# State-space convolution and gated MLP in one kernel: the opening stage in a new order, with the modulation vectors made by other matrix products

## The chip, the cores and the metric

The kernel runs on one core of one Trainium2 chip. The metric is the device time of one execution in microseconds, as the median of the runs. A core has a matrix engine (TensorE, PE in the profile, with its weight loads shown apart as PEld), a vector engine (VectorE, DVE), an activation engine (ScalarE, ACT), GpSimd (POOL) and SyncE (SP), whose queue issues most of the transfers here. Each engine runs its own instructions in order. Results of TensorE go to PSUM, from where VectorE or ScalarE takes them to SBUF.

## The reference

One sequence of L = 2048 positions and D = 640 channels goes through a block of two branches.

```python
mod = (silu(c) @ w_mod).reshape(6, 640)          # c is 1 x 640, w_mod 640 x 3840
sa, ca, ga, sb, cb, gb = mod
h = layernorm(x) * (1 + ca) + sa
P = exp(dt * A * l);  K = real(sum_n C * P * dB)  # 640 channels, 128 states, 2048 positions
x = x + ga * (causal_convolution(h, K) + h * Dskip)
h = layernorm(x) * (1 + cb) + sb
x = x + gb * ((silu(h @ w1) * (h @ w3)) @ w2)     # w1, w3: 640 x 1728
```

All of it is float32.

## The kernel before, in words

The program has three stages. In the **front** (0 to about 138 us of the span) everything is made that the convolution starts from. In the **rounds** (to about 380 us) the convolution's kernel for 16 channels at a time (a "step", 40 of them) is generated beside the Fourier transforms of u. Then follows the gated MLP, which is almost pure TensorE work. The change touches the front, and one addition in the first ten steps.

**What the front makes.** Eight blocks of the matrix `w_mod` (256 columns each, the last 128) give the vectors sa, ca and ga. A word `wl+i` of the list below loads block i, `ms+i` multiplies it with silu(c), and `mc+i` puts the result as columns (one channel per partition) into `cols`. In before, `ms` has silu(c) as the stationary operand and lets the 256 columns of the block stream past, in four column groups of TensorE at once. The result is a row, which VectorE copies to SBUF (`uk<-pm`), and `mc` turns it into columns by a product with a stationary piece of that row (`pm<-one`), which VectorE copies again (`cols<-pm`). From the columns `SA`, `SB`, `SC` and `SD` make the constant that the layer norm's shift adds to u (`rrow`, `shift`), and `MG`, `MH` make the gate.

The 16 tiles of x (`xl+j` loads one) get their layer norm (`LS`, statistics of two tiles on VectorE and four tiny operations on GpSimd; `LN`, the scaling, on ScalarE), and the first Fourier step (`U+j`, products of x with a constant matrix into two PSUM tiles `pu`). `V0+j` and `V1+j` take the two halves out, add the shift, and `V1+j` stores the tile's u to DRAM (`us<-u`). In before, for even j, TensorE adds the shift itself in the first half (products with `rrow`) and ScalarE copies that half; VectorE adds the shift in all others. The PSUM tile of the first half has one buffer, named Z.

For each step s: `PA`, `PQ` (products `pa<-r,lx`) make exponents, `XA`, `XQ` their exponential on ScalarE, `PH` phases on GpSimd (two steps at a time), `AB`, `CO`, `SI` their cosine and sine on ScalarE, `E1`, `E2`, `A1`, `A2` tables on VectorE, `kg` the kernel's pieces by TensorE into `pk`, `K` their way out on VectorE with Dskip added in one small operation (`pk<-pk,dz`) and the gate multiplied in, `pt` and `uk` its first Fourier step. `R1` to `R8` turn the parameters of channels 128 to 639 into logarithms and phases, with wide operations on VectorE and ScalarE; `dp` loads these parameters.

**The end of the front.** When all of u is in DRAM, eight transfers (`ul+0` to `ul+3`, `uk<-us`) bring the first 128 channels back with position and frequency exchanged, `st+10` multiplies them (`p<-uk,s`), ScalarE copies a part (`kc`), and VectorE's product `T` begins the rounds. `CL` closes the front's pools and loads the first constants of the rounds.

**What sets the order.** In the front each engine and SP's queue keep the order in which the list `FRONT` names the words, 264 of them; the list is written out by hand. The rounds follow a second list that stays as it is. A pool with one buffer adds waits: `pm` uses the PSUM banks pb and pk in turn, so a block's products wait until the copy of an earlier block has read its bank.

Of the kernel before, what the change touches and what calls it, by code (L numbers as in the profile page):

```python
# [17 lines left out]
P = 128  # L18
# [7 lines left out]
SPC = DC // SD  # L26
NS = D // SD
# [86 lines left out]
def tile_kernel(ctx: ExitStack, tc: tile.TileContext, a):  # L114
# [54 lines left out]
    V.memset(dz, 0.0)  # L169
    sc = kp.tile([P, KD], F32, name="sc")  # L170
# [17 lines left out]
    rrow = pm_.tile([P, D], F32, name="rrow")  # L188
# [168 lines left out]
    def mod_first(i):  # L357

        w = wm.pop(i)
        n = w.shape[2]  # L360
        pm = psS.tile([P, 512], F32, name="pm", tag=("pb", "pk", "pb", "pk", "pb", "pb", "pk", "pb")[i], bufs=1)
        mod_sums(w, pm)
        part = flat[2 * (i % 2)][:, 6 * D:]
        V.tensor_copy(part[:, :n], pm[:, :n])
        pms[i] = pm, part, n

    def mod_cols(i):

        pm, part, n = pms.pop(i)
# [6 lines left out]
    def shift_a():  # L376
# [114 lines left out]
    def u_products(j):  # L491
# [3 lines left out]
        for h in range(2):  # L495
            one = j % 2 == 0 and h == 0
            for q in range(2 if one else 0):
                for hh in range(2):
                    PE.matmul(pus[h][hh * 64:hh * 64 + 64, q, :320], c1[q * NA:q * NA + 1],
                              rrow[q * NA:q * NA + 1, hh * 320:hh * 320 + 320],  # L500
                              start=True, stop=False, tile_position=(q * NA, hh * 64))
            for q in range(2):
                r0 = (2 * h + q) * NA
                r = slice(r0, r0 + NA)
                for hh in range(2):
                    PE.matmul(pus[h][hh * 64:hh * 64 + 64, q, :320], s1r[r], x[r, hh * 320:hh * 320 + 320],
                              start=not one, stop=True, tile_position=(r0, hh * 64))

    def u_out(j, h):
# [108 lines left out]
    def kgen(s):  # L618
        E, A = EC.pop(s), AA.pop(s)
        pk = psS.tile([P, SD // 4, NB], F32, name="pk", tag="pk", bufs=1)  # L620
        for g in range(SD // 4):
            for st, x in enumerate((E, A)):
                for dq in range(4):
                    keep(PE.matmul(pk[dq * 32:dq * 32 + 32, g, :], x[:, g * 4 + dq, 1, :], x[:, g * 4 + dq, 0:3:2, :],
                                   start=(st == 0), stop=(st == 1), tile_position=(0, dq * 32)))
# [26 lines left out]
    def u_load(ch, i):  # L652

        fs = slice(i * 8, i * 8 + 8)
        for h in range(2):
            lo, hi = max(ch * DC, h * 320), min(ch * DC + DC, h * 320 + 320)
            if lo < hi:
                for c in range(2):
                    nc.sync.dma_start(uk[c * 64:c * 64 + 64, 0, fs, lo - ch * DC:hi - ch * DC],
                                      usr[h, c, :, fs, lo - h * 320:hi - h * 320])  # L660
# [200 lines left out]
    def small_loads():  # L861

        Q.dma_start(s1, a["s1"])
        Q.dma_start(i2, a["i2"])
        Q.dma_start(dz[NA - 8:P:NA], a["D"].rearrange("o (g q) -> (o q) g", q=4))

# [4 lines left out]
              "V1": lambda k: u_out(k, 1), "SA": once_only(shift_a), "SB": once_only(shift_b), "SC": once_only(shift_c),  # L871
# [6 lines left out]
              "ul": lambda k: u_load(0, k)}  # L878
    FRONT = (
# [695 lines left out]
```

## Time and profile before

| | us |
|---|---|
| runs | 950.4, 954.11, 955.71 |
| median | 954.11 |
| profiled execution | 954.98 |
| its span, first to last instruction | 952.8 |
| mean granted TensorE clock over the span | 0.955 |

All times below are those of the profiled execution, counted from the start of its span. Its own time is 2.2 us longer than the span, and 0.9 us above the median.

A row of the stretch view gives, for each engine, how long it was busy in that stretch and with how many instructions, then the clock granted to TensorE (1.00 is full speed), the share of the DMA engines and their rate. Timeline rows give start, duration, engine, operation, what is written from what, and in brackets how long the engine stood idle before it and who released it. One float32 matmul of the program stands in the trace as two records, so 15 products show as 30. The trace has no clock record before 28 us; the column shows 1.00 there for lack of one.

### The profile page before, as it was taken

The page shows a single profiled execution, that of the slowest core. Times are in us where ns is not written, and L with a number is a line of the kernel's source. Part 1 is how long each engine was busy: PE and PEld are TensorE (multiplying, and loading weights), DVE is VectorE, ACT ScalarE, POOL GpSimd, SP SyncE. Part 2 cuts the span into 40 slices and gives each one's busy share as a digit, 9 for nine tenths or more (in the row PEclk, how much of TensorE's full clock was granted, in tenths as well). Part 3 has the DMA queues.
Part 4 walks back from the last instruction along what each step waited for, and adds up shares of the span by engine and source line. Part 5 has one row for each costly group of instructions (what it writes and reads, how often), then busy time and mean ns, then how long its engine had stood idle before and what let it go on. Part 6 is the DMA issues. An engine that isn't in the chain of part 4 may idle for free.

```text
span 952.8 us, 20012 instructions
## 1 busy us (share of the span) xinstructions
PE 879.5 (92%) x7950; PEld 669.8 (70%) x7950; DVE 710.2 (75%) x1232; ACT 538.9 (57%) x737; POOL 269.0 (28%) x293
## 2 busy tenths in 40 slices
PE   3687979999998898999999999999999999999997
PEld 2453556666666664678888887578888888888786
DVE  5999979999999957577666665587976666664674
ACT  5877989999999632455333332466533333333332
POOL 3423345444544211133222201230242222200241
PEclk9867579999999998899999999999999999999999
DMA  8455397667675877782111116955321311123252
GB/s 267 149 170 195 153 230 208 170 180 195 195 224 153 231 219 255 203 262 83 42 56 56 56 62 191 248 199 171 126 70 55 111 56 56 56 82 98 97 189 87
DMA packets 104048, 140.68 MB, mean 148 GB/s; under 512 B 21044, under 2 KB 63156, under 8 KB 103956
## 3 DMA queue, kind: packets, MB, share of 16 engines
q1 hardware_dynamic: 93172, 113.58, 39.8%
q10 hardware_dynamic: 8480, 18.09, 5.9%
q0 software_dynamic: 2304, 7.74, 2.6%
q8 instruction: 62, 1.02, 0.4%
q14 instruction: 30, 0.25, 0.1%
HBM read 107.92 MB, written 31.46 MB: 146 GB/s over the span
## 4 chain that ended last, share of the span: by engine, by line
PE 68%; DVE 13%; ACT 7%; DMA 4%; SPq 3%; issue 3%; POOL 1%; ACTq 0%; DVEq 0%; POOLq 0%
PE ps L108 49%; PE p L108 6%; SPq L108 3%; PE pz L108 3%; PE pt L108 3%; PE pk L108 2%; PE pa L108 2%; DVE uk L108 2%; DVE u L108 2%; DVE st L108 2%; DVE E L108 1%; DVE A L108 1%; PE pu L108 1%; PE pm L108 1%; ACT A L108 1%
## 5 line engine op out<-in xcount | busy, mean ns | idle before, releaser
L108 DVE TENSOR_TENSOR s<-ps,s 128x512 f32<-128x512 f32 x138 | 94.8, 687 | 82.3 <-PE ps L108 81.6
L108 ACT CAST gh<-rw 128x640 fp32r<-128x640 f32 x87 | 63.3, 728 | 128.0 <-PE ps L108 86.4
L108 DVE TENSOR_TENSOR gl<-rw,gh 128x640 fp32r<-128x640 f32 x87 | 78.7, 904 | 69.1 <-ACT gh L108 69.1
L108 POOL TENSOR_TENSOR S<-rw 128x256 f32<-128x256 f32 x46 | 36.3, 791 | 234.3 <-DVE S0l L108 158.5
L108 PE MATMUL p<-uk,s 128*64 128x256 f32 x640 | 81.1, 397 | 16.3 <-DVE Y L108 4.0
L108 PE MATMUL ps<-xA,gh 128*128 128x512 f32 x280 | 87.6, 391 | 0.4 <-ACT xA L108 0.4
L108 PE MATMUL ps<-gh,uh 128*128 128x512 f32 x224 | 87.6, 391 | 0.0
L108 POOL TENSOR_TENSOR ph<-thi,iota 128x1376 int32<-128x1376 int32 x20 | 51.1, 2554 | 129.1 <-DVE A L108 114.0
L108 PE MATMUL ps<-gl,uh 128*128 128x512 f32 x224 | 87.3, 390 | 0.0
L108 PE MATMUL ps<-gh,ul 128*128 128x512 f32 x208 | 81.1, 390 | 0.0
L108 DVE TENSOR_TENSOR E<-A,cs 128x1024 f32<-128x1024 f32 (+1 forms) x80 | 76.5, 973 | 0.0
L108 PEld LDWEIGHTS p<-uk,s 128*64 128x64 f32 x640 | 46.6, 140 | 40.4 <-issue 7.7
L108 ACT ACTIVATE A<-pa 128x1024 f32<-128x1024 f32 (+1 forms) x80 | 64.6, 815 | 14.7 <-PE pa L108 14.6
L108 PEld LDWEIGHTS ps<-xA,gh 128*128 128x128 f32 x280 | 52.3, 188 | 12.9 <-ACT xA L108 1.0
L108 DVE TENSOR_TENSOR A<-A,ph 128x1024 f32<-128x1024 f32 x40 | 54.1, 1357 | 0.9
L108 PE MATMUL ps<-xA,gl 128*128 128x512 f32 x140 | 54.5, 390 | 0.0
L108 PE MATMUL pt<-s,K 128*64 128x128 f32 x640 | 47.4, 294 | 3.4 <-ACT uk L108 3.3
L108 PE MATMUL pz<-Y,i 64*128 64x128 f32 x640 | 47.3, 288 | 3.4 <-DVE T L108 1.8
L108 PEld LDWEIGHTS pz<-Y,i 64*128 64x128 f32 x640 | 39.6, 190 | 14.3 <-issue 8.4
L108 PE MATMUL pa<-r,lx 32*128 32x512 f32 (+1 forms) x160 | 34.5, 480 | 15.9 <-DVE u L108 9.0
L108 PEld LDWEIGHTS ps<-gl,uh 128*128 128x128 f32 x224 | 42.1, 188 | 9.0
L108 PEld LDWEIGHTS ps<-gh,uh 128*128 128x128 f32 x224 | 42.1, 188 | 8.9 <-DVE h L108 0.2
(211 smaller groups left out, 2181.1 us busy)
## 6 DMA issues: line engine op xcount, KB each, us to landing
rw<-in_w_dram ACTq DMA_DIRECT2D x44, 320.0 KB
us<-u SPq DMA_DIRECT2D x16, 640.0 KB
s<-in_s_dram SPq DMA_DIRECT2D x40, 256.0 KB
i<-in_i_dram SPq DMA_DIRECT2D x40, 256.0 KB
rw<-in_wg_dram SPq DMA_DIRECT2D x31, 320.0 KB
rw<-in_wu_dram SPq DMA_DIRECT2D x28, 320.0 KB
uk<-us SPq DMA_DIRECT2D x32, 256.0 KB
zs<-zt SPq DMA_DIRECT2D x32, 256.0 KB
```

What stands on the lines that cost most here:

```text
L108: ins = fn(*args, **kw)
```

## The change

The modulation blocks become stationary: for each 128 columns of a block and each of the five 128-row pieces of `w_mod`, one product has that 128x128 piece as its weights and one column of silu(c) as the moving operand. Ten such products per block (five for the last) leave the columns in PSUM directly; the row, its copy and the turning products go. The shift is added by VectorE alone in all 32 halves of u, and `rrow`, its copy and its products go; so does the word `SB`. In steps 0 to 9 Dskip is added by one more product into `pk` (`pk<-dz,dsel`) in place of VectorE's small addition. u is loaded in two pieces: `ul+0` to `ul+3` bring the positions of tiles 0 to 13, and a new word `ub` brings those of tiles 14 and 15, for all frequencies, in two transfers; the second set of round constants is loaded behind it. And the list is another one throughout.

```diff
-        mod_sums(w, pm)
-        part = flat[2 * (i % 2)][:, 6 * D:]
-        V.tensor_copy(part[:, :n], pm[:, :n])
-        pms[i] = pm, part, n
+        for b in range(n // P):
+            for k in range(KD):
+                PE.matmul(pm[:, b:b + 1], w[:, k, b * P:b * P + P], sc[:, k:k + 1], start=(k == 0), stop=(k == KD - 1))
+        pms[i] = pm, n
...
-        for b in range(n // P):
-            PE.matmul(pm[:, 256 + b:257 + b], part[:, b * P:(b + 1) * P], one4, start=True, stop=True)
-        V.tensor_copy(cols.rearrange("p s k -> p (s k)")[:, 2 * i:2 * i + n // P], pm[:, 256:256 + n // P])
+        V.tensor_copy(cols.rearrange("p s k -> p (s k)")[:, 2 * i:2 * i + n // P], pm[:, :n // P])
...
-        pr = sh["pr"] = psS.tile([P, 2, 512], F32, name="pr", tag="Z", bufs=1).rearrange("p a b -> p (a b)")
-        for k in range(KD):
-            PE.matmul(pr[:64, k * P:(k + 1) * P], r[:, k:k + 1].broadcast_to([P, 64]), ident, start=True, stop=True)
-
-    def shift_b():
-        V.tensor_copy(rrow[:64], sh["pr"][:64, :D])
...
-        if h == 0 and j % 2 == 0:
-            acopy(to, pu[:, :, :320])
-        else:
-            V.tensor_tensor(to, pu[:, :, :320], bc(shift, 1, 2), op=OP.add)
+        V.tensor_tensor(to, pu[:, :, :320], bc(shift, 1, 2), op=OP.add)
...
+        if s < EARLY:
+            keep(PE.matmul(pk[:, :, 0], dsel[:4], dz4[:4, s * 4:s * 4 + 4], start=False, stop=True,
+                           skip_group_check=True))
...
-        keep(V.tensor_tensor(pk[:, :, 0], pk[:, :, 0], dz[:, s * 4:s * 4 + 4], op=OP.add))
+        if s >= EARLY:
+            keep(V.tensor_tensor(pk[:, :, 0], pk[:, :, 0], dz[:, s * 4:s * 4 + 4], op=OP.add))
...
+    UB = 4 * 14
+
+    def u_last():
+
+        for c in range(2):
+            Q.dma_start(uk[c * 64 + UB:c * 64 + 64, 0], usr[0, c, UB:, :, :DC])
+        ahead[0, 1, "s2"] = stage2_load(1)
+        for i in range(2):
+            ahead[0, i, "i1"] = inverse1_load(i)
...
-              "ul": lambda k: u_load(0, k)}
+              "ul": lambda k: u_load(0, k, UB), "ub": lambda k: u_last()}
...
-        "PH+0 PA+0 xl+0 wl+0 PH+2 wl+4 ms+0 xl+7 wl+1 XA+0 ms+1 XA+1 PQ+0 xl+1 xl+6 mc+0 LS+0 XQ+0 wl+2 mc+1 "
+        "wl+3 xl+0 PA+0 PH+0 wl+2 xl+1 dp+0 wl+0 XA+0 XA+1 wl+1 wl+4 xl+5 ms+2 PQ+0 XQ+0 xl+4 mc+2 ms+3 XQ+1 "
```

How the queues move shows at three places. **TensorE, from its first instruction on** (`pT`, `pa` are exponents, `pm` the modulation blocks, `pr` and `ps` the shift). Before:

```order
L108 MATMUL pT<-ident,lt 128x128 x4
L108 MATMUL pa<-r_95,lx 128x512 x4
L108 MATMUL pm<-uk,sc 32x256 x4
L108 MATMUL pm<-uk,sc 32x128 x2
L108 MATMUL pm<-uk,sc 32x256 x4
L108 MATMUL pm<-uk,sc 32x128 x2
L108 MATMUL pa<-r_96,lx 128x256 x4
L108 MATMUL pm<-one_80,uk 128x1 x4
```

After, from the same place:

```order
L109 MATMUL pT<-ident,lt 128x128 x4
L109 MATMUL pa<-r_98,lx 128x512 x4
L109 MATMUL pm<-sc,uk 128x1 x10
L109 MATMUL pa<-r_99,lx 128x256 x4
L109 MATMUL pm<-sc,A 128x1 x10
L109 MATMUL pm<-sc,uk 128x1 x10
L109 MATMUL pa<-r_98,lx 128x512 x4
L109 MATMUL pm<-sc,A 128x1 x10
L109 MATMUL pm<-sc,uk 128x1 x10
L109 MATMUL pa<-r_99,lx 128x256 x4
L109 MATMUL pm<-sc,uk 128x1 x5
L109 MATMUL ps<-ident,u 64x128 x2
```

The blocks come in the order 2, 3, 0, 4, 1, 7 and then 6 and 5, and 55 products of one moving column now stand ahead of the shift's `ps`.

**VectorE, from the first modulation result on** (`cols<-pm` is a word `mc`, `st` and `mv` are layer norm statistics, `uk<-uk` 128x512 the `R` words, `E<-A,cs` tables). Before:

```order
L108 COPY uk<-pm 128x256 x2
L108 COPY cols<-pm 128x2
L108 BN_STATS st_218<-x 128x6 x2
L108 BN_AGGR mv_219<-st_218 128x2
L108 BN_STATS st_218<-x 128x6 x2
L108 BN_AGGR mv_219<-st_218 128x2
L108 COPY cols<-pm 128x2
L108 COPY uk<-pm 128x256
```

After:

```order
L109 COPY cols<-pm 128x2
L109 BN_STATS st_242<-x 128x6 x2
L109 BN_AGGR mv_243<-st_242 128x2
L109 BN_STATS st_242<-x 128x6 x2
L109 BN_AGGR mv_243<-st_242 128x2
L109 TENSOR_TENSOR uk<-uk 128x512 x6
L109 COPY cols<-pm 128x2 x2
L109 TENSOR_TENSOR E<-A,cs 128x16x64 x2
L109 SCALAR_TENSOR_TENSOR uk<-uk 128x512
L109 TENSOR_TENSOR uk<-uk 128x512
L109 SCALAR_TENSOR_TENSOR uk<-uk 128x512
L109 RECIPROCAL uk<-uk 128x512
```

The wide row copies are gone, `R1` to `R3` have moved up between the column copies, and each column copy still waits for its block on TensorE.

**SP's queue at the end of the front** (`us<-u` stores u, `uk<-us` loads it back, `s` and `i` are constants of the rounds). Before:

```order
L108 DMA us<-u 128x1280 x7
L667 DMA s_1253<-in_s_dram 128x512
L673 DMA i_1255<-in_i_dram 128x512
L667 DMA s_1257<-in_s_dram 128x512
L673 DMA i_1259<-in_i_dram 128x512
L659 DMA uk<-us 64x8x128 x8
```

After:

```order
L109 DMA us<-u 128x1280 x6
L657 DMA s_1264<-in_s_dram 128x512
L109 DMA uk<-us 56x8x128 x2
L109 DMA uk<-us 8x32x128 x2
L657 DMA s_1316<-in_s_dram 128x512
L663 DMA i_1318<-in_i_dram 128x512
L663 DMA i_1320<-in_i_dram 128x512
L109 DMA uk<-us 56x8x128 x6
```

One constant, the first 56 partitions of eight frequencies, and then the two transfers of the last tiles stand ahead of everything else.

More of the change, by code (lines that the diff above doesn't have):

```diff
@@ L26 @@
 SPC = DC // SD
+EARLY = SPC + 2
 NS = D // SD
@@ L169, in tile_kernel @@
     V.memset(dz, 0.0)
+    dz4 = kp.tile([P, D // 4], F32, name="dz4")
+    dsel = kp.tile([P, P], F32, name="dsel")
+    V.memset(dsel[:4], 0.0)
     sc = kp.tile([P, KD], F32, name="sc")
@@ L187, in tile_kernel @@
     pm_ = pre.enter_context(tc.tile_pool(name="pm_", bufs=1, side="right"))
-    rrow = pm_.tile([P, D], F32, name="rrow")
     shift = pm_.tile([P, D // 2], F32, name="shift")
@@ L361, in mod_first @@
         pm = psS.tile([P, 512], F32, name="pm", tag=("pb", "pk", "pb", "pk", "pb", "pb", "pk", "pb")[i], bufs=1)
[L362 to L365 removed]
+        for b in range(n // P):
+            for k in range(KD):
+                PE.matmul(pm[:, b:b + 1], w[:, k, b * P:b * P + P], sc[:, k:k + 1], start=(k == 0), stop=(k == KD - 1))
+        pms[i] = pm, n
     def mod_cols(i):
[L369 to L372 removed]
+        pm, n = pms.pop(i)
+        V.tensor_copy(cols.rearrange("p s k -> p (s k)")[:, 2 * i:2 * i + n // P], pm[:, :n // P])
     sh = {}
@@ L495, in u_products @@
         for h in range(2):
[L496 to L501, printed above, removed]
             for q in range(2):
@@ L506, in u_products @@
                     PE.matmul(pus[h][hh * 64:hh * 64 + 64, q, :320], s1r[r], x[r, hh * 320:hh * 320 + 320],
-                              start=not one, stop=True, tile_position=(r0, hh * 64))
+                              start=True, stop=True, tile_position=(r0, hh * 64))
     def u_out(j, h):
@@ L624, in kgen @@
                     keep(PE.matmul(pk[dq * 32:dq * 32 + 32, g, :], x[:, g * 4 + dq, 1, :], x[:, g * 4 + dq, 0:3:2, :],
-                                   start=(st == 0), stop=(st == 1), tile_position=(0, dq * 32)))
+                                   start=(st == 0), stop=(st == 1 and s >= EARLY), tile_position=(0, dq * 32),
+                                   skip_group_check=s < EARLY))
+        if s < EARLY:
+            keep(PE.matmul(pk[:, :, 0], dsel[:4], dz4[:4, s * 4:s * 4 + 4], start=False, stop=True,
+                           skip_group_check=True))
         PK[s] = pk
@@ L650, in tile_kernel, with u_load @@
     Pq, Yq, Zq = {}, {}, {}
-    def u_load(ch, i):
+    def u_load(ch, i, nb=NB):
         fs = slice(i * 8, i * 8 + 8)
@@ L658, in u_load @@
                 for c in range(2):
[L659 to L660 removed]
+                    Q.dma_start(uk[c * 64:c * 64 + nb, 0, fs, lo - ch * DC:hi - ch * DC],
+                                usr[h, c, :nb, fs, lo - h * 320:hi - h * 320])
     ahead = {}
@@ L911, in tile_kernel @@
     lx_out((0,))
+    V.tensor_copy(one4, one4m)
+    V.tensor_copy(dsel[:4, NA - 8:P:NA], toq[:4, NA - 8:P:NA])
     for word in FRONT:
@@ L916, in tile_kernel @@
             xw = fp.tile([P, 4 * D], F32, name="xw", bufs=1)
-            for i in range(2):
-                ahead[0, i, "s2"] = stage2_load(i)
-                ahead[0, i, "i1"] = inverse1_load(i)
+            ahead[0, 0, "s2"] = stage2_load(0)
         elif name in fronts:
```

4 lines of the change are left out of this document (2 added, 2 removed), and 26 rows, old and new, of the table FRONT.

## The prediction

> **What bounds the kernel now.** I read the page first. TensorE is the busiest engine over the whole span, but its first slices are not full, and the clock row shows it throttled there:
>
> ```profile
> PE 879.5 (92%) x7950; PEld 669.8 (70%) x7950; DVE 710.2 (75%) x1232; ACT 538.9 (57%) x737; POOL 269.0 (28%) x293
> PEclk9867579999999998899999999999999999999999
> ```
>
> The change lies in the first six slices of 23.8 us, so the table by stretch comes next (PE, PEld, DVE, ACT, POOL, then the granted clock):
>
> ```profile
> 16.39:30.00 13.61, 12.81 (x92) 7.89 (x92) 8.60 (x25) 11.89 (x11) 12.83 (x15) 1.00 0.93 296
> 16.39:121.75 105.36, 84.94 (x1088) 51.82 (x1088) 97.07 (x174) 86.73 (x87) 43.52 (x53) 0.71 0.50 174
> 121.75:138.06 16.31, 11.77 (x198) 8.83 (x198) 12.26 (x17) 13.27 (x15) 7.70 (x4) 0.69 1.09 233
> 138.06:300.00 161.94, 150.01 (x2865) 107.36 (x2862) 154.03 (x253) 152.36 (x155) 77.22 (x36) 1.00 0.68 192
> ```
>
> From the first exponent (16.39) to the last piece of u (121.75) VectorE is busy for 97.07 of 105.36 us and TensorE for 84.94: VectorE is the bound, idle for 8.3 us, of which 13.61 - 8.60 = 5.0 fall before 30 us. In the rounds behind 138.06, VectorE, ScalarE and TensorE are all over 92% busy in fixed orders, so I carry a shift of the front's end on one to one. The chain of waits shows that end:
>
> ```profile
> 120.22 1.54 DVE u L108 x2
> 121.79 3.61 DMA us<-u
> 126.17 7.25 DMA uk<-us
> 133.72 3.70 PE p L108 x16
> 138.06 0.70 DVE T L108
> ```
>
> The last store, the loads behind it and a slow `st+10` put 16.3 us between VectorE's last u and its `T`; only 12.26 of them are work for it.
>
> So the time is: VectorE's work up to the last u, plus its idle time, plus the tail. I take these in turn.
>
> **VectorE's work.** The groups of instructions up to 145 us give the prices (count, busy time, mean ns):
>
> ```profile
> L108 DVE TENSOR_TENSOR u<-pu,shift 128x640 f32<-128x640 f32 x24 | 18.7, 809 | 1.5 <-PE pu L108 1.5
> L108 DVE COPY uk<-pm 128x256 f32<-128x256 f32 x7 | 2.9, 417 | 3.9 <-PE pm L108 3.8
> L108 DVE COPY rrow<-pr 64x640 f32<-64x640 f32 x1 | 0.8, 807 | 0.0
> L108 DVE TENSOR_TENSOR pk<-pk,dz 128x4 f32<-128x4 f32 x11 | 1.8, 161 | 1.6 <-PE pk L108 1.5
> L108 DVE TENSOR_TENSOR K<-pk,gaT 128x256 f32<-128x256 f32 x11 | 4.7, 424 | 0.4
> L108 DVE BATCH_NORM_STATS2 st<-x 128x6 f32<-128x320 f32 x32 | 13.7, 469 | 0.0
> L108 DVE BATCH_NORM_AGGREGATE mv<-st 128x2 f32<-128x12 f32 x16 | 3.3, 209 | 1.0
> L108 DVE RECIPROCAL uk<-uk 128x512 f32<-128x512 f32 x1 | 3.4, 3352 | 0.0
> L108 ACT COPY u<-pu 128x640 f32<-128x640 f32 x8 | 5.5, 690 | 0.5 <-PE pu L108 0.4
> ```
>
> Gone: seven row copies and an eighth half as wide (7.5 x 0.417 = 3.1), `rrow` (0.8), and Dskip in the six steps taken out before the last u (6 x 0.16 = 1.0): 4.9 us. New: eight halves of u (8 x 0.77, half of the 1.54 of the pair above, = 6.2), and `K` of step 6, which moves ahead of the last u (0.4): 6.6. Net **+1.7**. ScalarE loses 8 x 0.69 = 5.5 us, but was idle for 18.6 of 105.36 us already; I count nothing for it. Dskip's ten products go on TensorE, which has 20 us of slack in this stretch, and cost nothing while it has; what they cost without it is in the third rival.
>
> One gain is hidden in the order. `SA` is a chain of tiny operations on five elements, and in before it falls beside GpSimd's wide `PH` of step 2:
>
> ```profile
> 28.60 3.54 POOL L108 TENSOR_TENSOR ph<-thi,iota 128x1376 int32<-128x1376 int32 x1
> 29.96 2.42 DVE L108 TENSOR_SCALAR cols<-cols 128x5 f32<-128x5 f32 x2
> 33.15 1.40 DVE L108 TENSOR_TENSOR cols<-cols 128x5 f32<-128x5 f32 x1
> 4.23 0.17 DVE L108 TENSOR_SCALAR sc<-sc 128x5 f32<-128x5 f32 x1 [3.10 <-ACT sc L108]
> ```
>
> Three operations take 3.8 us where 0.17 each would do (the 4.23 row). In the new list `PH` of step 2 stands behind `SA`. The gain lies between 0 (another chain falls beside `PH` instead) and 3.3; I take **-2.5**, nearer the row.
>
> **TensorE's first 45 us, and VectorE's idle time.** This is the term that decides. A product with a 128x128 stationary piece and one moving column is already in the trace, as `pm<-one`. In time order, TensorE's rows:
>
> ```profile
> 16.39 0.80 PE L108 MATMUL pa<-r,lx 32*128 32x512 f32 x4 [1.56 <-DVE lx L108]
> 19.82 0.58 PE L108 MATMUL pa<-r,lx 32*128 32x256 f32 x4
> 20.34 1.87 PE L108 MATMUL pm<-one,uk 128*128 128x1 f32 x8
> 20.34 1.78 PEld L108 LDWEIGHTS pm<-one,uk 128*128 128x128 f32 x8 [0.22 <-issue]
> 36.79 1.71 PE L108 MATMUL ps<-ident,u 128*64 128x128 f32 x12
> 43.16 0.61 PE L108 MATMUL pm<-one,uk 128*128 128x1 f32 x4
> 46.37 2.11 PE L108 MATMUL pu<-x,misc 32*64 32x320 f32 x16
> ```
>
> Its price is the weight load: 1.78 / 8 = 0.22 us a record at the early, slow clock, 0.61 / 4 = 0.15 at the fast one. A block is now 20 records: 4.45 us slow, 3.0 fast. Which clock holds? The table by stretches that follow the throttle's own steps of 3.41 us:
>
> ```profile
> 17.84:21.25 3.41, 3.41 (x29) 2.14 (x23) 0.85 (x2) 2.12 (x4) 3.25 (x4) 1.00 0.57 152
> 21.25:24.67 3.42, 3.42 (x23) 2.11 (x24) 3.14 (x11) 3.39 (x4) 3.26 (x3) 1.00 0.99 320
> 48.56:51.97 3.41, 3.41 (x16) 3.34 (x16) 3.38 (x3) 3.39 (x3) 0.00 (x0) 0.50 0.56 130
> 51.97:55.39 3.42, 2.41 (x32) 1.57 (x34) 3.38 (x8) 2.23 (x5) 0.00 (x0) 1.00 0.30 113
> 110.00:113.41 3.41, 3.41 (x34) 1.69 (x36) 3.41 (x5) 2.94 (x6) 1.31 (x3) 0.50 0.48 192
> ```
>
> TensorE was busy without a gap in the first two (their 1.00 is only the missing record), and the products in them still cost 0.22. It was as busy in the step from 110.00 at 0.50. The step from 48.56, all 128-column products through the whole array, was followed by 1.00. So a full busy row does not release the clock; columns that stream through the array seem to, and the new products stream one. I take the slow clock for all eight blocks.
>
> Then I walk TensorE's new order. Block 2 ends at 17.1 + 4.45 = 21.6, exponents 0.58, block 3 at 26.6, block 0 at 31.0, exponents 0.80, block 4 at 36.3, block 1 at 40.7, exponents, block 7 (half) at 43.5, the shift's `ps` at 45.5. VectorE beside it, with 0.3 us from an end on TensorE to a copy: idle from 16.6 to 21.9 (5.3). `LS+0` is 4 x 0.43 + 2 x 0.2 = 2.1 and `R1` 3.9 (six wide operations at 0.66), until 28.2; idle until block 0 at 31.3 (3.1). Two tables at 1.2 and `R2`, `R3` (0.66 x 4 + 3.35 = 6.0) last until 39.8; idle until 41.0 for block 1 (1.2). `SA`, `SC`, `LS+2`, `A1+1` and the shift's copy fill until 47.4, when the first product of u stands. The two first tiles of u hold TensorE until 50.4, block 6 until 54.9, the third tile until 57.0, block 5 until 61.4: VectorE waits 1.5 for that tile and 3.0 for block 5. That is 14.1; I add 1.4 for two small waits behind it, for the gate and the next u: 15.5 us, against 5.0 until 30 us and 0.5 from there to 60 in before. With the later 2.8 kept on both sides: **+10.0**. Bounds: +0.5 when the clock is released early (first rival), +13 when each of the three largest waits is one more us.
>
> The `dp` load, 1536 KB, now stands ahead of three blocks in SP's queue. Transfers ran at 296 GB/s in the first stretch above, so it is some 5 us; block 0 is wanted at 26.6, and 5 MB ahead of it are in by about 20. Nothing is added.
>
> **The tail.** The last store still has to land (3.6 of the chain). In before eight loads and four constants then share the DMA engines, and the first two loads take 7.25. In after two transfers of the last tiles go first, and `ul+0` is issued before them. If they take as long as now, the gain is 0; if they are hidden, VectorE's own work of 12.26 - 0.4 - 0.5 = 11.3 is what is late next, and the gain is 16.3 - 11.3 = 5.0. I take **-3.3**, nearer the second, since little is queued ahead. `ul+1` to `ul+3` gain nothing; they wait behind the last tiles on SP. [...]
>
> **The sum.** +1.7 - 2.5 + 10.0 - 3.3 = +5.9 us. The profiled execution took 954.98, so 960.9; it lay 0.9 above the median of the runs, and against that I forecast **960.0**. The bounds of the terms make 956 to 965 of this case. A measurement of this kernel can tell about 0.5%, 4.8 us, from no change.
>
> **Rivals.**
>
> *The clock is released.* For it: TensorE's queue is without a gap from 16.4 to 50 us. [...] Then blocks cost 3.0: block 0 ends at 28.2, VectorE waits 5.3 + 0.3, no other block is late, and the idle term is +0.5. Sum -3.6: 950.5. Chance 0.16.
>
> *The gains reach their ends.* `SA` brings 3.3, the tail 5.0, and the two late waits (4.5 with the small ones 5.9) are covered by loads and tables that come out earlier: idle 9.6 - 5.5 = +4.1. Sum 1.7 - 3.3 + 4.1 - 5.0 = -2.5: about 952. Against it: the waits for blocks 6 and 5 follow from TensorE's order. Chance 0.11.
>
> *VectorE becomes the only way out of PSUM.* The bank Z holds one half of u; ScalarE took eight of sixteen. If TensorE, at the slow clock and with Dskip's products in its queue, waits for Z and VectorE then for TensorE, each of those eight costs another 0.81: +6.5, 966.5. It decides once TensorE's slack of 20 us is gone; the new blocks alone take 33 us (150 records at 0.22). Chance 0.13.
>
> **How the numbers follow.** The main case keeps 0.60: slower by over 0.5% in 0.42 (from 958.9 on), within in 0.17, faster in 0.01. The clock's case gives faster 0.06, within 0.10; the gains' case faster 0.03, within 0.08; the third slower 0.13. Together: faster 0.10, within 0.35, slower 0.55. The range of 951 to 967 leaves out about half of the clock's case, the upper part of the third and the main case's ends, some 0.18.
>
> **What would show it.** Right: the clock at 0.50 from the first record to beyond 60 us, weight loads of the blocks at 0.22, the last `cols` copy of a block near 61, VectorE's last u near 131, and `T` some 13 us behind it. Wrong: records at 0.15 before 30 us (then the idle term falls), `SA` still slow beside GpSimd, or a tail of 16 us as now. The forecast as a whole is wrong if VectorE's last u comes before 123.

## The result, and the profile after

The changed kernel took 961.82 us (median of six runs, 957.73 to 962.58) against 953.91 us for the kernel before on the same chip (six runs, 950.4 to 955.71): a ratio of 1.0076, with a 95% interval of 1.0059 to 1.0092. The forecast was 960.0. Its profiled execution has a span of 960.0 us, 7.2 more than before.

From the page, the busy time of each engine and the clock row in 40 slices of 24 us:

```profile
PE 890.0 (93%) x7920; PEld 689.5 (72%) x7920; DVE 708.7 (74%) x1223; ACT 539.9 (56%) x733; POOL 273.0 (28%) x293
PEclk9999679999999999999999999999999999999999
```

The clock row looks better than before in its first slices, and is not: the trace has no clock record before 84.27 us, and the row shows full speed where there is none. The speed must be read from durations. TensorE's rows in time order (start, duration, tile, count):

```profile
17.11 4.43 PE L109 MATMUL pm<-sc,uk 128*128 128x1 f32 x20
35.63 4.41 PE L109 MATMUL pm<-sc,uk 128*128 128x1 f32 x20
52.57 1.37 PE L109 MATMUL pu<-x,misc 32*64 32x320 f32 x16
53.87 4.43 PE L109 MATMUL pm<-sc,uk 128*128 128x1 f32 x20
59.73 0.44 PE L109 MATMUL pk<-A 128*32 128x64 f32 x8
80.83 3.68 PE L109 MATMUL pT<-ident,lt 128*128 128x128 f32 x16
85.29 0.29 PE L109 MATMUL pk<-A 128*32 128x64 f32 x8
```

A block costs 4.43 us, 0.22 a record, the same from the first to the last. Eight products of `pk` take 0.44 at 59.73 and 0.29 at 85.29, behind the `pT` products. In the kernel before the same eight take 0.44 in a stretch granted 0.50:

```profile
56.69 0.44 PE L108 MATMUL pk<-A 128*32 128x64 f32 x8
55.39:58.80 3.41, 3.41 (x76) 2.12 (x79) 3.27 (x9) 3.39 (x3) 1.09 (x3) 0.50 0.83 277
```

So TensorE of the changed kernel ran at half speed through the `pT` products.

The table by stretch (PE, PEld, DVE, ACT, POOL), cut at VectorE's last u and at the first `T`:

```profile
16.38:124.72 108.34, 94.47 (x1118) 70.87 (x1118) 94.94 (x169) 86.87 (x84) 47.71 (x52) 0.92 0.48 166
124.72:142.32 17.60, 10.79 (x133) 8.21 (x133) 11.85 (x14) 13.55 (x14) 8.08 (x5) 0.61 1.02 200
```

VectorE's last u ends at 124.72, 3.0 us later than before; the tail behind it takes 17.60 us, 1.3 more than the 16.31 of before. VectorE's own rows, with the idle time ahead of an operation and its releaser in brackets:

```profile
16.31 1.69 DVE L109 COPY dsel<-misc 4x4 f32<-4x4 f32 x1
21.58 0.16 DVE L109 COPY cols<-pm 128x2 f32<-128x2 f32 x1 [3.58 <-PE pm L109]
30.72 0.16 DVE L109 COPY cols<-pm 128x2 f32<-128x2 f32 x1 [3.07 <-PE pm L109]
40.07 0.23 DVE L109 COPY cols<-pm 128x2 f32<-128x2 f32 x2 [1.00 <-PE pm L109]
40.81 0.37 DVE L109 TENSOR_SCALAR cols<-cols 128x5 f32<-128x5 f32 x2
54.53 0.82 DVE L109 TENSOR_TENSOR u<-pu,shift 128x640 f32<-128x640 f32 x1 [1.42 <-DMA us<-u]
58.33 0.16 DVE L109 COPY cols<-pm 128x2 f32<-128x2 f32 x1 [0.57 <-PE pm L109]
142.32 0.69 DVE L109 TENSOR_TENSOR T<-p,kc 128x512 f32<-128x512 f32 x1 [3.68 <-ACT kc L109]
158.08 0.69 DVE L109 TENSOR_TENSOR T<-p,kc 128x512 f32<-128x512 f32 x1 [1.47 <-ACT kc L109]
```

The third `T` of the kernel before:

```profile
152.47 0.68 DVE L108 TENSOR_TENSOR T<-p,kc 128x512 f32<-128x512 f32 x1
```

The waits for blocks are the first, second, third and fifth bracket, 8.2 us together. The first `T` stands 4.26 us later than before, but the third 5.61 (158.08 against 152.47), and from there the distance holds: it is 5.57 at 170.72. The first and the third product of the rounds, on TensorE:

```profile
137.98 3.68 PE L109 MATMUL p<-uk,s 128*64 128x256 f32 x16 [2.77 <-ACT cs L109]
155.42 1.95 PE L109 MATMUL p<-uk,s 128*64 128x256 f32 x16 [1.36 <-DMA s<-in_s_dram]
```

The first bracket names ScalarE's cosine, which ends at 137.71. The landing records of the transfers name another candidate: the two loads of the last tiles, the second of which lands at 137.63. The table, made from the semaphore records of the traces, gives, for the loads ahead of the first product, when they were issued, when their last piece landed, and how often they moved their semaphore.

```text
                       issued   landed  moves
before  last store     121.79   125.40   16
        u, 64 x 8 freq 125.48   132.08   16
        u, 64 x 8 freq 126.17   133.42   16
after   last store     124.75   129.05   16
        u, 56 x 8 freq 125.73   131.30   15
        u, 56 x 8 freq 127.07   133.73   15
        u,  8 x 32     129.11   134.76    9
        u,  8 x 32     129.42   137.63    9
```

So there are three things to test: the half-speed blocks, the tail, and what makes the third product late.

### The profile page after: what moved, and what is told of

It is laid out like the page before. It is cut to its first block, busy times and chain, and to the rows that moved or that the text cites. A ratio compares the mean times of both kernels' runs of the same rounds, so it can differ in the third digit from the quotient of the medians.

```text
span 960.0 us, 19931 instructions
## 1 busy us (share of the span) xinstructions
PE 890.0 (93%) x7920; PEld 689.5 (72%) x7920; DVE 708.7 (74%) x1223; ACT 539.9 (56%) x733; POOL 273.0 (28%) x293
## 4 chain that ended last, share of the span: by engine, by line
PE 67%; ACT 11%; DVE 9%; DMA 5%; SPq 4%; issue 3%; POOL 1%; DVEq 0%; ACTq 0%; POOLq 0%
PE ps L109 49%; PE p L109 6%; SPq L109 4%; PE pm L109 3%; ACT cs L109 3%; DMA s<-in_s_dram 3%; PE pz L109 2%; PE pt L109 2%; PE pk L109 2%; ACT A L109 2%; PE pa L109 1%; ACT L109 1%; ACT ph L109 1%; DVE st L109 1%; PE pu L109 1%
## 5 line engine op out<-in xcount | busy, mean ns | idle before, releaser
L109 PE MATMUL p<-uk,s 128*64 128x256 f32 x640 | 84.1, 408 | 18.3 <-DMA s<-in_s_dram 6.5
L109 PEld LDWEIGHTS pt<-s,K 128*64 128x64 f32 x640 | 38.5, 149 | 16.5 <-ACT uk L109 11.1
```

What stands on the lines that cost most here:

```text
L109: ins = fn(*args, **kw)
```

## The experiments

Each kernel was timed against runs of the kernel before on its own chip, whose median lay between 953.9 and 956.2 us; so the ratios are compared, and 0.001 is about 1 us. The changed kernel's ratio is 1.0076.

**Streaming 128 columns in place of one.** The copy then reads every 128th column of the result.

```diff
-                PE.matmul(pm[:, b:b + 1], w[:, k, b * P:b * P + P], sc[:, k:k + 1], ...)
+                PE.matmul(pm[:, b * 128:b * 128 + 128], w[:, k, b * P:b * P + P], sc[:, k:k + 1].broadcast_to([P, 128]), ...)
```

> The changed kernel with one edit: silu(c)'s column is repeated 128 times as the moving operand of the modulation products, so that each streams 128 columns through the array in place of 1; the result stands in 128 equal columns, of which one is copied. Theory A (the clock is released by columns that stream, and a product costs its weight load anyway): TensorE is released to full speed before 30 us instead of 84, a record of the blocks falls from 0.22 to 0.15 us or less, VectorE's waits for blocks fall from 8.2 to 3 or 4 us, its last u comes 3 to 5 us earlier, and the time falls by 3 to 5 us, to 957 to 959. Rival B (busy time counts, or the clock keeps its own pace): the records stay at 0.22 or grow, the clock stays at half speed beyond 60 us, and the time is 961 to 964. Rival C (the clock is released, but the waits for blocks were slack of the list): records at 0.15, last u less than 1 us earlier, time within 1 us of 961.8.

Measured: 958.41 us, ratio 1.0033 (1.0013 to 1.0054). The clock records of before and after each last 3.41 us or a whole multiple of it, but for the last of each. Two steps of that length of this run in the table by stretch:

```profile
17.88:21.29 3.41, 3.41 (x18) 3.41 (x17) 0.36 (x1) 1.51 (x2) 2.56 (x3) 1.00 1.15 313
21.29:24.70 3.41, 3.41 (x32) 3.16 (x31) 2.88 (x9) 2.64 (x3) 0.60 (x2) 1.00 0.89 332
```

A stretch of the same length in the changed kernel:

```profile
17.84:21.25 3.41, 3.41 (x18) 3.41 (x17) 0.16 (x1) 1.32 (x2) 2.36 (x3) 1.00 1.15 312
```

TensorE's rows of the run:

```profile
17.35 4.36 PE L109 MATMUL pm<-sc,uk 128*128 128x128 f32 x20
21.96 2.50 PE L109 MATMUL pm<-sc,A 128*128 128x128 f32 x20
24.30 2.40 PE L109 MATMUL pm<-sc,uk 128*128 128x128 f32 x20
```

The first block costs the same with 128 columns as with one, 4.36 and 4.43, and the weight loads are busy for 4.17 and 4.34 of that: they set the price. Both kernels show TensorE and the weight loads busy without a gap, with the same counts, in the stretch from 17.9; only the columns differ. In the next step this run has 32 records in place of 18; the changed kernel goes on at 0.22 a record. So between these two kernels the busy time that the profile shows does not decide: behind the same 3.41 us without a gap, the records fell to 0.12 with 128 columns and stayed at 0.22 with one. Full-speed blocks cost 2.4 us, 0.12 a record; VectorE's waits for blocks fall from 8.2 to 3.5, all of it for the first. Theory A holds, with the gain in time as it has it, though the last u comes only 2.4 us earlier.

**u in one piece.** The two transfers of the last tiles go, and the loads are 64 partitions wide.

```diff
-            Q.dma_start(uk[c * 64 + UB:c * 64 + 64, 0], usr[0, c, UB:, :, :DC])
-              "ul": lambda k: u_load(0, k, UB), ...
+              "ul": lambda k: u_load(0, k), ...
```

> The changed kernel with u loaded back in one piece (64 partitions a transfer, behind the last store), the two transfers of the last tiles gone, and the second set of constants still behind the first two loads. Theory A (the first product of the rounds waits for the two 8-partition transfers of all frequencies, which land at 137.63): the two loads land about 2 + 2.6 us behind the landing of the last store at 129.05, that is near 134; that product starts at 134 to 135 instead of 137.98, T at 138 to 139.5 instead of 142.32, the time falls by 3 to 4 us. Rival B (as the chain of waits names it, that product waits for ScalarE's cosine, which ends at 137.71): it still starts near 138, and the time stays within 1 us.

Measured: 958.78 us, ratio 1.0033 (1.0010 to 1.0055). The two loads were issued at 129.36 and 130.06 and landed at 133.29 and 134.67. The first product and the first `T`:

```profile
135.26 3.68 PE L109 MATMUL p<-uk,s 128*64 128x256 f32 x16
139.60 0.69 DVE L109 TENSOR_TENSOR T<-p,kc 128x512 f32<-128x512 f32 x1 [0.83 <-DMA uk<-us]
```

ScalarE's cosine of this run:

```profile
135.92 1.91 ACT L109 ACTIVATE cs<-cs 128x2048 f32<-128x2048 f32 x1
```

With VectorE's last u where it was, `T` comes 2.7 us earlier. The product starts before the cosine does, so in the changed kernel it waited for the loads, not for the cosine that the chain named: theory A, though `T` is 0.1 later than its bound. By the ratios the two-piece load is a loss of about 0.4%. This profile does not show where all of it comes from: by the third `T` (157.28 against 158.08) 0.8 us of the 2.7 is left, since the third product waits 1.90 us for its constant, and the profiled execution, at 963.83 us, is 5 us above the run's median.

**The last piece cut to 8 frequencies.** The early loads stay 56 partitions wide; of the last tiles only what the first product reads comes ahead.

```diff
-            Q.dma_start(uk[c * 64 + UB:c * 64 + 64, 0], usr[0, c, UB:, :, :DC])
+            Q.dma_start(uk[c * 64 + UB:c * 64 + 64, 0, :8], usr[0, c, UB:, :8, :DC])
-              "ul": lambda k: u_load(0, k, UB), ...
+              "ul": lambda k: u_load(0, k, NB if k else UB), ...
```

> The changed kernel, but the two transfers of the last tiles bring only the first 8 frequencies (all that the first product of the rounds reads); the other 24 come with the other loads, each in one piece. [...] Rival B (ScalarE's chain is the bound): product near 138, time within 1 us. Rival C (the split itself costs, whatever its size, by its fixed time of landing): T no earlier than with whole loads.

Measured: 957.67 us, ratio 1.0015 (0.9996 to 1.0034). The two small transfers were issued at 127.55 and 127.86 and landed at 130.79 and 131.24, 3.4 us after the issue against 8.2 in the changed kernel. VectorE's first `T`:

```profile
137.03 0.68 DVE L109 TENSOR_TENSOR T<-p,kc 128x512 f32<-128x512 f32 x1
```

The chain of waits before its third:

```profile
142.61 7.72 DMA s<-in_s_dram
150.47 3.56 PE p L109 x16
154.72 0.70 DVE T L109
```

The first `T` is 5.3 us earlier, and VectorE does not wait ahead of it any more. Its last u also came 1.5 us earlier here, with the clock released at 61.58 in place of 84.27, which the edit did not touch; the tail is 3.8 us shorter. The front up to the last u is the same in the changed kernel, in the run with u in one piece, in this run and in the next. In the first two the clock was released at 84.27 and 84.39, and the last u ends at 124.7 and 124.8; in the other two it was released at 61.58 and 61.78, and the last u ends at 123.2 and 123.5. So a last u that differs by up to 1.7 us between two profiles need not come from an edit, and a part of the 2.4 us of the 128 columns can be of this kind.

The size of the last two transfers was the fault of the split. But the small split is not shown to be better than none: the product starts 10.3 us behind the last u here and 10.4 with u in one piece, 13.3 in the changed kernel, and the intervals of the two ratios overlap. `T` gains on the whole load only as the last u is earlier and as the product takes 1.95 us at the full clock, where it took 3.68. So rival C is not excluded.

Why the large pieces landed so late is not shown beyond their size. Their landing records differ from those of the other loads (8 partitions moved their semaphore 9 times, 56 moved it 15 times, 64 moved it 16 times), but no view here tells the DMA engines apart.

The third `T`, at 154.72, is 17.69 us behind the first, 15.76 in the changed kernel, and there 1.9 us of the gain is lost to a constant that landed 7.72 us after its issue.

**That constant ahead of xw and the next u.** On the kernel of the run above:

```diff
     front[0] = False
+    ahead[0, 2, "s2"] = stage2_load(2)
```

> The kernel of the run before with the smaller last transfers, and one load moved: the constant s of the third product of the rounds (128x512, 256 KB) is issued behind u's loads and ahead of xw and the next chunk's u, instead of behind them. There the first T of the rounds stood at 137.03, but the third at 154.72, 17.69 us later against 14.41 in the kernel before, with the constant issued at 142.61 and landed at 150.33. Theory A (that constant, late in SP's queue, took back what the tail gained): it lands before 147, the third T stands 14.4 to 15.5 us behind the first, the time falls by 2 to 3 us against that run, to 954.5 to 956. Rival B (another thing of the round is late next): the distance stays over 16.5 and the time within 1 us of 957.7.

Measured: 955.73 us, ratio 0.9997 (0.9983 to 1.0011). The constant was issued at 135.71 and landed at 144.39; no wait for it is left:

```profile
150.62 1.95 PE L109 MATMUL p<-uk,s 128*64 128x256 f32 x16
153.29 0.69 DVE L109 TENSOR_TENSOR T<-p,kc 128x512 f32<-128x512 f32 x1
```

The third `T` is 15.95 us behind the first (137.34): less than 17.69, a little more than theory A's bound, and still 1.5 more than the 14.41 of the kernel before. With the constant early and the split cut down, the changed kernel is as fast as the kernel before.

**The tail alone, on the kernel before.** u whole; one constant ahead of it instead of four, and the constant of the third product early.

```diff
-            for i in range(2):
-                ahead[0, i, "s2"] = stage2_load(i)
-                ahead[0, i, "i1"] = inverse1_load(i)
+            ahead[0, 0, "s2"] = stage2_load(0)
...
+              "ul": lambda k: (u_load(0, k), later_constants() if k == 0 else None)}
+    ahead[0, 2, "s2"] = stage2_load(2)
```

> The kernel before with its tail alone changed: u whole, but only the first constant stands ahead of it, the other three behind the first two loads, and the constant of the third product behind u's loads. Nothing of the modulation, the shift or the list. Theory A (what the tail waits for in the kernel before is the four constants ahead of u): the first product starts at 130 to 131 in place of 133.72, T at 134 to 136 in place of 138.06, the time falls by 2 to 4 us. Rival B (VectorE's and ScalarE's own work, 12 to 13 us of the 16, is the bound at once): T within 1.5 us of 138, time within 1 us of the kernel before.

Measured: 954.56 us beside 956.17, ratio 0.9982 (0.9960 to 1.0005). The first and the third `T`:

```profile
135.45 0.68 DVE L108 TENSOR_TENSOR T<-p,kc 128x512 f32<-128x512 f32 x1
...
150.71 0.69 DVE L108 TENSOR_TENSOR T<-p,kc 128x512 f32<-128x512 f32 x1 [0.78 <-ACT kc L108]
```

The profile shows `T` 2.6 and 1.8 us earlier, as theory A has it, with the first product at 131.56, half a us behind its range. But 0.9 of it stands at the last u already (120.88 against 121.76), which the edit does not touch, so the tail itself is 1.7 us shorter; and the interval of the ratio includes 1. That the order of the constants is worth something is likely, not shown; it needs no split.

**The new products in the old order.** The kernel before with the modulation of the change, and nothing else of it.

```diff
-        mod_sums(w, pm)
-        V.tensor_copy(part[:, :n], pm[:, :n])
...
+        for b in range(n // P):
+            for k in range(KD):
+                PE.matmul(pm[:, b:b + 1], w[:, k, b * P:b * P + P], sc[:, k:k + 1], start=(k == 0), stop=(k == KD - 1))
```

> The kernel before, in its own order, with one part of the change alone: the modulation by 128x128 stationary pieces and one-column products; the rows, their copies and the turning products are gone. Theory A (a block costs 4.45 us at half speed, and the clock stays there): the clock is not released before 60 us, VectorE saves 3.1 us of copies but waits longer for blocks, 5 to 9 us against 4.8; last u within 121 to 125; time 953 to 958. Rival B (the old list hides the blocks): VectorE's waits stay near 5, last u 3 us earlier, time 951 to 952. Rival C (the clock is released as before since other products stream between the blocks): records at 0.15 from 38 us on, time 950 to 952.

Measured: 961.06 us, ratio 1.0053 (1.0032 to 1.0073). A row of VectorE's waits:

```profile
DVE cols L108 <- PE pm L108: 15.1, 5, 5.2
```

TensorE's first blocks in time order:

```profile
17.48 8.69 PE L108 MATMUL pm<-sc,uk 128*128 128x1 f32 x40
...
31.71 8.69 PE L108 MATMUL pm<-sc,A 128*128 128x1 f32 x40
```

Each row holds two blocks. At 4.35 us each they cost what they cost in the changed kernel, the first clock record is at 63.76, and VectorE waits 15.1 us for them. Theory A's mechanism holds, but the waits are larger than any theory had; the last u ends at 130.8. One-column products are a loss of 0.5% in the old order.

**The old products in the new order.** The changed kernel with rows, their copies and turning products.

```diff
-                PE.matmul(pm[:, b:b + 1], w[:, k, b * P:b * P + P], sc[:, k:k + 1], start=(k == 0), stop=(k == KD - 1))
+        mod_sums(w, pm)
+        V.tensor_copy(part[:, :n], pm[:, :n])
...
+            PE.matmul(pm[:, 256 + b:257 + b], part[:, b * P:(b + 1) * P], one4, start=True, stop=True)
```

> The changed kernel and its list, with the modulation computed as in the kernel before: rows by streaming the block, copied by VectorE, turned by one-column products. Theory A (the half-speed blocks of one-column products are what VectorE waits for): the waits for blocks, 8.2 us, fall to 3 or 4, VectorE's copies add 3.1, the clock is released before 60 us, the last u comes 1 to 2 us earlier, time 959.5 to 961. Rival B (the order of the list makes the waits): waits stay near 8, and the copies come on top: last u 3 us later, time 964 to 966.

Measured: 967.36 us, ratio 1.0115 (1.0088 to 1.0143). VectorE's waits for them:

```profile
DVE uk L109 <- PE pm L109: 5.6, 6, 1.6
DVE cols L109 <- PE pm L109: 4.8, 3, 2.5
```

Theory A falls: the waits are 10.4 us, not 3 or 4, and the copies come on top, as theory B says. The last u ends 3.9 us later than in the changed kernel, and by the ratio the time is 3.7 us more, within theory B's range. That a block with two steps on TensorE and one on VectorE makes both engines wait in turn would explain it, but is not shown: the clock was at full speed here for one step from 33.7 and then at half speed to 88.3, which can have a part in it.

**The shift as before, in the new order.** ScalarE copies the first half of the even tiles, TensorE adds the shift there.

```diff
+        for k in range(KD):
+            PE.matmul(pr[:64, k * P:(k + 1) * P], r[:, k:k + 1].broadcast_to([P, 64]), ident, start=True, stop=True)
...
-        V.tensor_tensor(to, pu[:, :, :320], bc(shift, 1, 2), op=OP.add)
+        if h == 0 and j % 2 == 0:
+            acopy(to, pu[:, :, :320])
+        else:
+            V.tensor_tensor(to, pu[:, :, :320], bc(shift, 1, 2), op=OP.add)
```

> The changed kernel with the shift as in the kernel before: for even tiles TensorE adds it in the first half (products with a row of it, made once) and ScalarE copies that half; VectorE adds it in the other 24 halves. Theory A (VectorE's work up to the last u sets the end of the front): VectorE loses 8 x 0.78 and gains one copy of 0.81, so its last u comes 4 to 5 us earlier, the time 3 to 5 us less than 961.8. Rival B (ScalarE, over 91% busy from 92 us on, becomes the bound by the 8 x 0.69 = 5.5 us that it takes back): last u within 1.5 us, time 960 to 963. Rival C (slower: TensorE at half speed has no room for the extra products early): time over 963.

Measured: 972.73 us, ratio 1.0179 (1.0158 to 1.0199). Waits up to 146 us (total, times, longest):

```profile
ACT u L109 <- PE pu L109: 15.8, 4, 7.3
PE pt L109 <- ACT uk L109: 10.9, 2, 6.4
DVE u L109 <- PE pu L109: 9.4, 4, 7.2
```

Theories A and B fall. VectorE has 5.4 us less to do, and the kernel is about 10 us slower than the changed one. ScalarE waits for u's products, TensorE for ScalarE, VectorE for TensorE. Theory C has the sign, and blames TensorE's half speed; the last run below tests that.

**Dskip by VectorE**, in all steps, on the changed kernel.

```diff
-EARLY = SPC + 2
+EARLY = 0
```

> The changed kernel with Dskip added by VectorE in every step, as in the kernel before; TensorE's ten products into pk are gone. Theory A (VectorE is the bound of the front, the products are free on TensorE): VectorE gains 7 x 0.16 = 1.1 us of work up to its last u, which comes 0.5 to 1.5 us later; the time grows by 0.5 to 2 us over 961.8. Rival B (the products stand in TensorE's chain to K, where they cost 0.5 us each at half speed, and VectorE waits there): last u comes 0 to 1.5 us earlier, time 960 to 962.

Measured: 964.28 us beside 955.99, ratio 1.0070 (1.0047 to 1.0093). The last two u stand at 122.91 against 123.17, 0.3 us earlier, which fits theory B. But the clock was released at 63.13 here; beside the run with the last piece cut, released at 61.58, the last u ends 1.3 us later (124.45 against 123.18), which fits theory A. The ratio is that of the changed kernel within its interval and decides neither. Ten products on TensorE in place of ten small VectorE operations are worth nothing that shows in the time.

**Three edits together**, on the changed kernel, with the diffs shown above: 128 columns, the cut last piece, the constant early.

> Three edits on the changed kernel together: the modulation products stream 128 equal columns, the transfers of the last tiles bring 8 frequencies, and the constant of the third product goes ahead of xw. Theory A (they mend waits in different places: blocks early, loads at the end): first T at 133.5 to 135.5 (137.3 with the last two alone, 2.9 earlier by the first), third T at 149 to 151, time 2 to 3 us less than with the last two alone, ratio to the kernel before 0.996 to 0.998. Rival B (the tail is then bound by the last store and the DMA engines, so the early gain is given back): first T 136 or later, third T over 152, ratio 0.999 or more.

Measured: 950.75 us beside 955.99, ratio 0.9942 (0.9920 to 0.9964), faster than the kernel before and the changed one. Its first and third `T`:

```profile
135.74 0.68 DVE L109 TENSOR_TENSOR T<-p,kc 128x512 f32<-128x512 f32 x1
...
150.72 0.69 DVE L109 TENSOR_TENSOR T<-p,kc 128x512 f32<-128x512 f32 x1 [0.72 <-ACT kc L109]
```

The early gain arrives at the rounds: 2.6 us earlier at the third `T` than without the 128 columns. The first `T` is 0.2 us outside of theory A's range, and the ratio is better than it.

**128 columns and the tail, in the old order**: the kernel before with the new products, their moving column repeated 128 times, and the tail's diff as above.

> The kernel before in its own order with two edits: the modulation by stationary pieces, but streaming 128 equal columns, and the tail's loads as in the run with the tail alone. Theory A (in the old order the new products cost by the half-speed clock, not by their form): the clock is released near 21 us, VectorE's waits for blocks fall from 15.1 to 5 to 8, VectorE saves 3.1 us of row copies, the first T comes 0 to 3 us earlier than the 135.45 of the tail alone, ratio to the kernel before 0.994 to 0.998. Rival B (form and order cost, whatever the clock: 20 records a block in TensorE's queue ahead of u's products): waits stay over 10, first T at 138 or later, ratio over 1.0.

Measured: 955.44 us beside 955.99, ratio 0.9996 (0.9975 to 1.0016). VectorE's waits up to 150 us:

```profile
DVE cols L108 <- PE pm L108: 5.6, 2, 5.0
DVE E L108 <- ACT cs L108: 3.6, 1, 3.6
...
DVE u L108 <- ACT cs L108: 1.4, 1, 1.4
```

Theory A is half right: the clock is released at 20.95 and the waits for blocks are 5.6 in place of 15.1. But the 3.1 us of copies saved turn into 5.0 us of waits for ScalarE's cosines, and the first `T`, at 135.92, is no earlier than with the tail alone; the third, at 153.82, is 3.1 us later. In the old order ScalarE is late next, and the new products bring nothing that shows; in the new order they do.

**The shift as before, with the clock released.** The edit of the run with ScalarE's copies, on the three edits together, with the diff shown there.

> The kernel with the three edits (128 columns streamed, smaller last transfers, the constant first), with ScalarE copying the first half of the even tiles as in the kernel before. On the changed kernel this edit cost about 11 us, with ScalarE waiting 15.8 us for products of u and VectorE 9.4. Theory A (the new list has no room on ScalarE at these places: each copy stands behind exponents and tables, and TensorE and VectorE wait for it in turn): it costs 7 to 12 us here too, ratio to the kernel before 1.002 to 1.007. Rival B (the half-speed clock made TensorE late for the extra products): with the clock released early it costs under 3 us or gains up to 4, ratio 0.990 to 0.998.

Measured: 968.36 us beside 954.20, ratio 1.0141 (1.0116 to 1.0166), 0.0199 above the three edits alone. Waits up to 146 us:

```profile
ACT u L109 <- PE pu L109: 11.8, 4, 7.3
DVE u L109 <- PE pu L109: 11.4, 4, 7.2
```

It costs more here, not less: theory A, beyond its range. So the half speed of the blocks is not why; in this order ScalarE's copies, with the products that go with them, make the in-order engines wait for one another. Whether another order has room for them was not tried.

## Why the prediction was right

The time came out as forecast, 1.8 us above, and its main case happened: the blocks at half speed. The sum of the terms was 5.9; the span grew by 7.2. But three of the four steps missed by more than this, in both directions, and that they cancel is luck. The prediction had VectorE's last u near 131 and `T` some 13 us behind it; they came at 124.72 and 17.6 us behind. A tail of 16 us as before was one of its own signs of being wrong, and the last u lay 1.7 us from the 123 that it had set as the bound for the whole.

- **VectorE's work up to the last u**: forecast +1.7 - 2.5 = -0.8; measured 94.94 - 97.07 = -2.1. The +1.7 was right: the same rows give +1.9. The gain of the tiny operations was sized too small: on five elements they cost 0.8 us in place of 5.9, so 5.1 where the range ended at 3.3, since the gate's one, 1.60 us in before, fell to 0.11 as well as `SA`'s. Against that, a copy of 4x4 elements, `dsel`, which the prediction put at nothing, took 1.69 us, though in the idle time ahead of the first block's copy.
- **Idle time**: forecast +10.0; measured 108.34 - 94.94 = 13.4 against 8.3, so +5.1. The price of a block, 4.45, and the slow clock beyond 60 us were right. The walk along TensorE's order was right to 0.7 us up to block 1 (40.0 against 40.7) and the waits for blocks 0 and 1 (3.07 and 1.00, forecast 3.1 and 1.2). It failed behind that: a tile of u was sized by a row of 2.11 us and took 1.37, three of them before block 5, so block 5 ended at 58.3 in place of 61.4, and VectorE waited 0.57 for it, not 3.0. The 1.5 us ahead of the third tile came (1.42), but its row names the store of an earlier u as what ended it, not TensorE. The wait for the first block was 3.58, not 5.3, since `dsel` filled 1.7 of it.
- **The tail**: forecast -3.3; measured +1.3. This step failed in sign. The value was taken "nearer the second, since little is queued ahead"; what mattered was the two transfers themselves, 8.2 us from the issue of the second to its landing. The miss was 4.6. Cut to 8 frequencies they landed in 3.4 us, and the tail shrank to 13.8 us, 2.5 below that of before; with u in one piece it was 14.8. Of the 0.9 us between these two, 0.2 lies ahead of the first product and the rest behind its start, where it ran at the full clock. So it is not shown that a small last piece brings more than none.
- **One to one into the rounds**: wrong by 2.9 us. 1.35 of it came between the first and the third `T`, where the third product's constant is queued behind the late loads (1.36 us in its bracket). Early, it made no wait, but the distance was still 15.95, so the constant is not shown to be all of it. The other 1.6 came later, 0.6 of it between the 23rd and the 31st `T`; the throttle's records show dips at 295.9 and 323.2 there, to 0.50 for 3.41 us each, that the kernel before does not have. What causes these dips stays open.

Together: -4.9 (idle) - 1.3 (work) + 4.6 (tail) + 2.9 (rounds) on 5.9 gives 7.2. These terms are read from one execution of each kernel, and the last u of the same front moved by up to 1.7 us between profiles. The forecast's sign rested on the half-speed blocks, and these were shown: 128 columns give back 0.43%. An equal part, 0.43% by the times of the run with u in one piece, goes with the split load, which the forecast had as a gain.

**The rivals.** The clock was not released before 84.27, and the rival's reason was weak, as the prediction's own stretches said: TensorE's queue is without a gap from 16.4 to 45.8 us, and the blocks in it stay at 0.22 us a record. The gains' case did not happen. The third rival had it that VectorE as the only way out of PSUM would cost 6.5 us, TensorE waiting for VectorE and VectorE then for TensorE. The waits of the changed kernel up to 146 us show 3.9 us of the first and 0.5 of the second:

```profile
PE pu L109 <- DVE u L109: 3.9, 4, 1.3
...
DVE u L109 <- PE pu L109: 0.5, 1, 0.5
```

The runs that gave ScalarE its eight halves back cost about 10 and 19 us, so in this order the edit that the rival blamed is one that the kernel cannot do without.

## What to carry to other kernels

A queue of products with one moving column can be busy without a gap and stay at half speed, here at 0.22 us a record for all eight blocks; where the weight load set the price, repeating the moving column cost nothing here and nearly halved it (4.43 to 2.40 us a block). The speed is read from the durations, since the clock row showed full speed where it had no record, here up to 84.27 us. Of a transfer split off to land early, look at the size (here 8.2 us from issue to landing with 32 frequencies, 3.4 with 8), at when it lands, and at what is queued behind it two steps later, before the gain is counted, and try it against no split at all. When parts of a change are tested one by one, expect the order of in-order queues to be part of each: here the new products lose 0.53% in the old order, the old products 1.15% in the new, and the two together 0.76%, less than their sum.

## What was not expected of the hardware

- The same 128x128 weight load with one or with 128 moving columns costs 0.22 us a record at half speed; with 128 it fell to 0.12 after one step of 3.41 us, with one it stayed at 0.22 through all eight blocks, to 58.3 us.
- The clock was released at 84.27 and 84.39 us in two profiles and at 61.58 and 61.78 in two others, with the same front in all four.
- The second of two transfers of 8 partitions by 32 frequencies took 8.2 us to land, behind two of 56 partitions, where the second of two of 64 partitions by 8 frequencies, each with twice the bytes, took 4.6 in the run with u in one piece.
- A VectorE copy of 4x4 elements took 1.69 us beside a wide GpSimd operation, and ended with it (18.00 and 17.98).
